# GLA recurrence and max-out MoE in one kernel: where w2·wo is summed, where unit 1's MoE stands, and how the last output is cut

## The chip, the cores and the metric

The kernel runs on one core of a Trainium2 chip. The metric is the time of one execution in device microseconds (us). Seven executions of the kernel before took 147.97 to 148.68 us, with a median of 148.49 us.

## What is computed

There are two stages. A gated recurrence runs over 768 time steps for 4 batches and 8 heads of 48 elements; its output, laid out as 3072 tokens of 384 elements, goes through a max-out block with 1024 hidden elements:

```python
for t in range(S):
    state = alpha[:, :, t, :, None] * state + np.einsum('bhd,bhe->bhde', k[:, :, t], v[:, :, t])
    y[:, :, t] = np.einsum('bhd,bhde->bhe', q[:, :, t], state)
x = y.transpose(0, 2, 1, 3).reshape(B * S, H * D)
out = np.maximum(x @ w1, x @ w2) @ w_out
```

All inputs and the output are float32.

## The kernel before

**Units.** The 3072 tokens are cut into 12 units of 256 tokens: unit u is block d = u // 4 of batch b = u % 4, and it holds two chunks (cc = 0, 1) of 128 tokens. Units 0 and 1 load q, k and v in another layout than the rest (`PAIRED`), which makes their loads fewer and some of their operations different. A unit's recurrent state comes from unit u - 4, so units 0 to 3 begin without one.

**The recurrence of a unit** goes through these helpers, each of which issues instructions at once on the engines named:

- `ln` (L190, ACT): the logarithm of alpha into one of three tiles `lg`.
- `sumd`, `sumc` (L215, L227, PE): sums over tokens of those logarithms, by matmuls with masks, into two PSUM tiles `cs` (tags g0, g1).
- `expm`, `expp`, `expd` (ACT): exponentials of the sums, into `Em`, back into `cs`, and into `de`.
- `kmul` (POOL) and `qmul` (DVE): k times `Em`, q times `cs`.
- `turn` (L291, PE, then a DVE copy at L301 or L303 into `qk`): eight 128x128 transposes for each chunk.
- `kvmm` (L305, PE), `kvsum` (DVE), `state` (POOL): the state's update.
- `pmm` (L338, PE) into two tiles `pp`, `pmask` (L347, DVE): the products of k and q in a chunk, and the causal mask over them, out of PSUM into `pt`.
- `ystate`, `yin` (PE), with two copies into `xn` on ACT (L388): the unit's output.
- `vcast` (L197): v to fp16, two casts on POOL (L205), two on ACT (L207), in units 0 and 1 two more on POOL (L209).

**The MoE of a unit.** max(h1, h2) is computed as relu(h1 - h2) + h2. So w12 = w1 - w2 is made once in quarters (`wsub`, L474, DVE), and w2o = w2 @ w_out is made once: `wcast` (L470, ACT and POOL) turns the two halves of w_out into fp16 `wo16`, `wturn` transposes w2, `wmul` (L455, 12 matmuls for each half of the hidden elements) sums into three PSUM tiles `wqs`, and `wout` (L466, three ACT copies) stores it. A unit then needs

- `xturn` (L390): six transposes and a DVE copy into `xt` (L399);
- `hid(u, f2)` (L401) for f2 = 0 to 3: six matmuls of 256 columns (L410) into a PSUM tile, and a relu into `gT`, on ACT (L415) or DVE (L417);
- `outp(u, n)` (L419) for each half n of 128 tokens: `outx`, three matmuls of 384 columns (x times w2o, L429), and `outg`, eight of 384 columns (`gT` times `wo16`, L436), then an ACT copy into `outs` (L439) and the store.

`dummies` (L478) issues matmuls on zeros, which no result uses.

**What sets the order.** `tc.manual_schedule()` (L484): from there each engine executes its instructions in the order of the calls, L487 to L640. Waits for data and for buffers are put in by the framework. An instruction that waits holds back everything behind it on its engine. All loads and stores are issued by SyncE (SP) in one queue, in order of the calls.

**Buffers.** PSUM has eight banks: tags m and pp with two each, g0 to g3 with one each. Tag m serves `dummies`, `wturn`, `hid`, `outx` and two of the three `wqs`; g0 and g1 serve `cs` and `turn`, g2 and g3 `kvmm`, `ystate`/`yin` and `xturn`. A tile on a tag waits until the readers of the tile before it are done.

**The order around the change** (L529 to L640): unit 0's `xturn`; unit 1's `turn`, `pmm`, `pmask` with `wmul(0)`, `wmul(1)` and `wout` between; the four `hid` of unit 0, with `wsub` and `dummies` between; `vcast(1)`; `ln(2)`; `outp(0, 0)`; unit 1's state, `sums(2)`, `exps(2)`; `outp(0, 1)`; unit 1's output, `turn(2)`, `xturn(1)`, `vcast(2)`, the four `hid` of unit 1, `ln(3)`. Then a loop over u = 2 to 11, where from u = 3 on the MoE of unit u - 1 stands between the steps of unit u; in the pass u = 2 only `outp(1, 0)` and `outp(1, 1)` do. The MoE of unit 11 follows the loop.

Of the kernel before, what the change touches and what calls it, by code (L numbers as in the profile page):

```python
# [8 lines left out]
FP16 = mybir.dt.float16  # L9
FP32 = mybir.dt.float32  # L10
# [5 lines left out]
def kernel(  # L16
# [27 lines left out]
    nc = tc.nc  # L44
    B, H, S, D = q.shape
    C = 128
    HP = H // 2
    P64 = 64
    ND2 = S // (2 * C)
    NU = B * ND2  # L50
    NT, DM = out.shape
    DFF = moe_w1.shape[1]
    NF = DFF // 128
# [12 lines left out]
    st = {}  # L66
# [33 lines left out]
    def load(u):  # L100
        load_a(u)
        if u in PAIRED:
            load_fat(u, "kf", k)
            load_fat(u, "qf", q)
        else:
            load_kq(u, 0)
            load_kq(u, 1)
        load_v(u)
# [77 lines left out]
    def new(tag, shape, dtype, bufs, name):  # L186
        return psp.tile(shape, dtype, tag=tag, bufs=bufs, name=name)


    def ln(u):  # L190
        X = st[u]
        X["lg"] = LG[u % NB]
        nc.scalar.activation(  # L193
            out=X["lg"][:, :, :, 0:D], in_=X["af"].rearrange("p h j d -> p j h d"), func=ACTF.Ln
        )
# [94 lines left out]

    def turn(u, cc):  # L291
        X = st[u]
        tp = new(f"g{cc}", [128, 2, HP, C], FP16, 1, "tp")
        for n, src in ((1, X["kn"][cc]), (0, X["qn"][cc])):
            for j in range(HP):
                nc.tensor.transpose(tp[:, n, j, :], pair(src, j), ident)  # L296
        if cc == 0:
            X["qk"] = gp.tile([128, 2, 2 * HP, C], FP16, tag="qk", bufs=2, name="qk")
        if u in PAIRED:
            o = X["qk"].rearrange("p c n (j t) -> p j n c t", j=2)[:, cc]  # L300
            nc.vector.tensor_copy(out=o, in_=tp.rearrange("p n h (c t) -> p (n h) c t", c=2))  # L301
        else:
            nc.vector.tensor_copy(out=X["qk"][:, cc], in_=tp.rearrange("p n h t -> p (n h) t"))  # L303
# [34 lines left out]
    def pmm(u, cc):  # L338
        X = st[u]
        qk = X["qk"][:, cc].rearrange("p (n h) t -> p n h t", n=2)  # L340
        X["pa", cc] = pa = [new("pp", [128, HP, C], FP32, 2, "pp") for _ in range(2)]
        for j in range(HP):
            for a in range(2):
                r = slice(64 * a, 64 * a + D)
                nc.tensor.matmul(pa[a][:, j, :], lhsT=qk[r, 1, j, :], rhs=qk[r, 0, j, :], start=True, stop=True)  # L345

    def pmask(u, cc):  # L347
        X = st[u]
        pt = X["pt", cc] = gp.tile([128, 2, HP, C], FP16, tag="pt", name="pt")
        for a in range(2):  # L350
            nc.vector.tensor_mul(  # L351
                out=pt[:, a], in0=X["pa", cc][a], in1=um.unsqueeze(1).to_broadcast([128, HP, C])
            )
# [36 lines left out]
    def xturn(u):  # L390
        X = st[u]
        xp = new("g2", [128, ND, 2, C], FP16, 1, "xp")
        for cc in range(2):
            xf = X["xn"][:, cc].rearrange("p j a d -> p (j a d)")
            for ds in range(ND):
                o = xp[:, ds].rearrange("p j (c t) -> p c j t", c=2)[:, cc]
                nc.tensor.transpose(o, xf[:, ds * 128 : (ds + 1) * 128], ident)  # L397
        X["xt"] = mp.tile([128, ND, 2, C], FP16, tag="xt", bufs=3, name="xt")
        nc.vector.tensor_copy(out=X["xt"], in_=xp)  # L399

    def hid(u, f2, on_act=None):  # L401
        X = st[u]
        if f2 == 0:
            X["gT"] = mp.tile([128, NF, 2 * C], FP16, tag="gT", name="gT")
        gT = X["gT"]
        hp = new("m", [128, 2, 2 * C], FP32, 2, "hp")
        for n in range(2):
            f = 2 * f2 + n
            for ds in range(ND):
                nc.tensor.matmul(  # L410
                    hp[:, n, :], lhsT=w12[:, ds, f * 128 : (f + 1) * 128],
                    rhs=X["xt"][:, ds].rearrange("p n t -> p (n t)"), start=(ds == 0), stop=(ds == ND - 1),
                )
        if f2 != 3 if on_act is None else on_act:
            nc.scalar.activation(out=gT[:, 2 * f2 : 2 * f2 + 2, :], in_=hp, func=ACTF.Relu)  # L415
        else:
            nc.vector.tensor_relu(out=gT[:, 2 * f2 : 2 * f2 + 2, :], in_=hp)  # L417

    def outp(u, n):  # L419
        outx(u, n)  # L420
        outg(u, n)
# [6 lines left out]
        for ds in range(ND):  # L428
            nc.tensor.matmul(op, lhsT=X["xt"][:, ds, n, :], rhs=w2o[:, ds, :], start=(ds == 0), stop=False)  # L429

    def outg(u, n):
        X = st[u]
        d, b = divmod(u, B)
        op = X["op"]
        for f in range(NF):
            nc.tensor.matmul(  # L436
                op, lhsT=X["gT"][:, f, n * C : (n + 1) * C], rhs=wo16[:, f, :], start=False, stop=(f == NF - 1)
            )
        nc.scalar.copy(out=X["outs"][:, n, :], in_=op)  # L439
        t0 = b * S + d * 2 * C  # L440
        dst = out[t0 : t0 + 2 * C, :].rearrange("(p j) d -> p j d", j=2)
        if u == NU - 1:
            nc.sync.dma_start(out=dst[:, n], in_=X["outs"][:, n])
        elif n == 1:
            nc.sync.dma_start(out=dst, in_=X["outs"])

    def wturn(ds):
        wt = new("m", [128, NF, 128], FP16, 2, "wt")
# [3 lines left out]

    wqs = []

    def wmul(n):  # L455

        if n == 0:
            wqs.extend([new("m", [128, DM], FP32, 2, "wq") for _ in range(2)] + [new("g3", [128, DM], FP32, 1, "wq")])
        for ds in range(ND):
            for f in range(4 * n, 4 * n + 4):  # L460
                nc.tensor.matmul(  # L461
                    wqs[ds], lhsT=w2T[:, f, ds * 128 : (ds + 1) * 128], rhs=wo16[:, f, :],
                    start=(f == 0), stop=(f == NF - 1),
                )

    def wout():  # L466
        for ds in range(ND):
            nc.scalar.copy(out=w2o[:, ds, :], in_=wqs[ds])

    def wcast(n):  # L470
        nc.scalar.copy(out=wo16[:, 4 * n : 4 * n + 2], in_=wof[:, 4 * n : 4 * n + 2])
        nc.gpsimd.tensor_copy(out=wo16[:, 4 * n + 2 : 4 * n + 4], in_=wof[:, 4 * n + 2 : 4 * n + 4])

    def wsub(n):  # L474
        f = slice(n * DFF // 4, (n + 1) * DFF // 4)
        nc.vector.tensor_sub(out=w12[:, :, f], in0=w1f[:, :, f], in1=w2f[:, :, f])

    def dummies(n):  # L478

        warm = new("m", [128, 512], FP32, 2, "warm")  # L480
        for _ in range(n):
            nc.tensor.matmul(warm, lhsT=wz[:, 0:128], rhs=wz, start=True, stop=True)  # L482
# [44 lines left out]
    qmul(1, 0)  # L527
    qmul(1, 1)
    xturn(0)  # L529
    turn(1, 0)  # L530
    dummies(2)
    turn(1, 1)
    wcast(0)
    pmm(1, 0)
    pmask(1, 0)
    wmul(0)
    wcast(1)
    wsub(0)
    pmm(1, 1)
    pmask(1, 1)  # L540
    wmul(1)
    wout()

    load(3)
    hid(0, 0, True)
    wsub(1)
    hid(0, 1, True)
    wsub(2)
    dummies(2)
    hid(0, 2, True)  # L550
    wsub(3)
    dummies(2)
    vcast(1)
    hid(0, 3, True)
    load(4)
    ln(2)
    outp(0, 0)
    kvmm(1, 0)
    kvmm(1, 1)
    kvsum(1, 0)  # L560
# [1 line left out]
    kvsum(1, 1)  # L562
    sums(2)
    exps(2)
    outp(0, 1)
    for cc in range(2):
        kmul(2, cc)
    for cc in range(2):
# [2 lines left out]
    yin(1)  # L571
    turn(2, 0)
    turn(2, 1)
    dummies(1)
    xturn(1)
    dummies(1)
    vcast(2)
    for f2 in range(4):
        hid(1, f2)
    ln(3)  # L580
    load(5)


    for u in range(2, NU):
        nxt = u + 1 < NU
        if u + 4 < NU:
            load(u + 4)
        kvmm(u, 0)
        pmm(u, 0)
        kvsum(u, 0)  # L590
        pmask(u, 0)
        state(u, 1)
        if more(u):
            kvmm(u, 1)
        if u > 2:
            hid(u - 1, 0)
            hid(u - 1, 1)
            if nxt:
                sumd(u + 1)
            hid(u - 1, 2)  # L600
        else:
            outp(1, 0)
            sumd(u + 1)
        if nxt:
            sumc(u + 1)
            expm(u + 1, 0)
            expp(u + 1, 0)
            expm(u + 1, 1)
        if more(u):
            kvsum(u, 1)  # L610
        pmm(u, 1)
        ystate(u)
        pmask(u, 1)
        if u > 2:
            hid(u - 1, 3, True)
        if nxt:
            expp(u + 1, 1)
            expd(u + 1)
            for cc in range(2):
                kmul(u + 1, cc)  # L620
                qmul(u + 1, cc)
            state(u + 1, 0)
        outp(u - 1, 0 if u > 2 else 1)
        yin(u)
        if nxt:
            turn(u + 1, 0)
            turn(u + 1, 1)
        if u > 2:
            outx(u - 1, 1)
        xturn(u)  # L630
        if nxt:
            vcast(u + 1)
        if u + 2 < NU:
            ln(u + 2)
        if u > 2:
            outg(u - 1, 1)
    for f2 in range(4):
        hid(NU - 1, f2)
    outp(NU - 1, 0)
    outp(NU - 1, 1)  # L640

# [1 line left out]
_INS = ['q', 'k', 'v', 'alpha', 'moe_w1', 'moe_w2', 'moe_w_out']  # L643
# [26 lines left out]
```

## Time and profile before

| what | us |
|---|---|
| median of 7 executions | 148.49 |
| the profiled execution, its own time | 148.6 |
| its span, first to last instruction | 146.9 |
| PE busy in the span | 136.3 (93%) |
| ACT, DVE, POOL busy | 97.2, 87.4, 56.5 |
| matmuls on zeros (L482, 33 of them) busy | 11.4 |
| first `kvmm` of the passes u = 2, 3, 4, 5 | 42.25, 49.91, 59.88, 69.64 |
| the last quarter of w1 lands | 27.40 |
| last matmul ends / last store issued / landed | 143.50 / 144.03 / 145.89 |

Lines of the timeline give the start and the length of a group of instructions on an engine, the engine, the source line, the operation, what it writes and reads, its size and how often it stands there; in brackets stands the idle time of the engine before it and what ended it. Matmuls overlap, so that a group's length holds the last one's way through the array (about 0.16 us after the next one could start). The chain of waits follows the end of the execution back from one instruction to what released it.

### The profile page before, as it was taken

Reading aid. Unit: us, or ns where it says so; the run is one execution under the profiler, and the core shown is the slowest. Engines: PE = TensorE matmul, PEld = TensorE weight load, DVE = VectorE, ACT = ScalarE, POOL = GpSimd, SP = SyncE. Lnnn points to the kernel's source line nnn. Section 1 sums busy time; section 2 is a strip of 40 time slices with the busy share of each in tenths; the row PEclk is TensorE's granted clock in tenths of the full one; section 3 lists DMA queues with packets and bytes.
Section 4 is the critical chain, followed back from the end, with each engine's and each line's share of the span. In section 5 each row is a group of like instructions: output and inputs, shape, how many; then the busy total and the mean of one; then the engine's idle time right before and its main releaser. Section 6 shows DMA issues by size and latency. Waiting matters only on the chain.

```text
span 146.9 us, 4239 instructions
## 1 busy us (share of the span) xinstructions
PE 136.3 (93%) x1681; PEld 97.6 (66%) x1681; DVE 87.4 (60%) x180; ACT 97.2 (66%) x199; POOL 56.5 (38%) x111
## 2 busy tenths in 40 slices
PE   6849978999899999999999999999999999998990
PEld 2335645666776787767877777678777777775750
DVE  6046988904648876756767867566675756570010
ACT  3467452777566878688687886887879768654511
POOL 7491252055405438154181371541913617310000
PEclk9995999999999999999999999999999999999999
DMA  4999999969969995799899999969969969120202
GB/s 111 270 372 306 311 365 341 224 115 220 178 117 258 158 286 100 145 220 168 178 285 159 283 170 240 224 111 262 197 112 278 171 116 345 61 107 4 107 12 95
DMA packets 76339, 28.58 MB, mean 195 GB/s; under 512 B 71712, under 2 KB 74528, under 8 KB 76320
## 3 DMA queue, kind: packets, MB, share of 16 engines
q1 hardware_dynamic: 76320, 28.32, 83.4%
q8 instruction: 13, 0.21, 0.6%
q14 instruction: 6, 0.05, 0.1%
HBM read 23.59 MB, written 4.72 MB: 193 GB/s over the span
## 4 chain that ended last, share of the span: by engine, by line
PE 86%; ACT 4%; DVE 4%; DMA 3%; issue 1%
PE hp L410 23%; PE op L436 21%; PE op L429 8%; PE tp L296 7%; PE pp L345 5%; PE cs L237 4%; PE wq L461 3%; PE ya L381 3%; PE warm L482 3%; DMA af<-in_alpha_dram 3%; PE xp L397 3%; PE kv L318 2%; DVE qk L303 2%; PE cs L223 2%; PE ya L369 1%; ACT cs L252 1%
## 5 line engine op out<-in xcount | busy, mean ns | idle before, releaser
L410 PE MATMUL hp<-xt,w 128*128 128x256 f16 x288 | 37.2, 273 | 0.8 <-DVE xt L399 0.6
L415 ACT ACTIVATE gT<-hp 128x512 f16<-128x512 f32 x46 | 27.4, 596 | 14.4 <-PE hp L410 13.7
L351 DVE TENSOR_TENSOR pt<-pp,um 128x512 f16<-128x512 f32 x48 | 30.9, 686 | 9.3 <-PE pp L345 8.8
L436 PE MATMUL op<-wo,gT 128*128 128x384 f16 x192 | 35.1, 326 | 0.0
L285 POOL TENSOR_TENSOR kn<-kf,Em 128x384 f16<-128x384 f32 x24 | 23.4, 997 | 23.7 <-ACT Em L247 23.7
L410 PEld LDWEIGHTS <-w 128*128 128x128 f16 x288 | 26.1, 97 | 6.1 <-issue 2.2
L436 PEld LDWEIGHTS <-gT 128*128 128x128 f16 x192 | 18.4, 98 | 11.3
L277 POOL TENSOR_TENSOR sb<-tm,dd 128x192 f16<-128x192 f32 x20 | 10.1, 506 | 38.2 <-DVE tm L331 23.4
L439 ACT COPY outs<-op 128x384 f32<-128x384 f32 x24 | 11.5, 478 | 16.9 <-PE op L436 16.7
L289 DVE TENSOR_TENSOR qn<-qf,cs 128x384 f16<-128x384 f32 x24 | 12.3, 550 | 12.2 <-ACT de L257 12.2
L331 DVE TENSOR_TENSOR tm<-kv,sb 64x192 f32<-64x192 f32 x32 | 11.3, 353 | 9.1 <-PE kv L318 6.9
L429 PE MATMUL op<-w2o,xt 128*128 128x384 f16 x72 | 15.6, 326 | 0.0
L303 DVE COPY qk<-tp 128x1024 f16<-128x1024 f16 x20 | 12.9, 686 | 4.3 <-PE tp L296 4.3
L205 POOL CAST v<-vf 64x384 f16<-64x384 f32 x24 | 12.0, 501 | 6.5 <-DMA vf<-in_v_dram 5.7
L247 ACT ACTIVATE Em<-cs 128x384 f32<-128x384 f32 x24 | 11.6, 485 | 4.0 <-PE cs L237 4.0
L207 ACT CAST v<-vf 64x384 f16<-64x384 f32 x24 | 12.2, 510 | 1.4 <-DMA vf<-in_v_dram 0.9
L482 PE MATMUL warm<-wz 128*128 128x512 f16 x33 | 11.4, 452 | 1.3 <-DVE halves L149 1.3
L193 ACT ACTIVATE lg<-af 128x768 f16<-128x768 f32 x12 | 10.1, 843 | 3.3 <-DMA af<-in_alpha_dram 3.1
L252 ACT ACTIVATE cs<-cs 128x384 f32<-128x384 f32 x24 | 11.8, 493 | 0.0
L296 PE MATMUL tp<-ident,kn 128*128 128x128 f16 x96 | 9.2, 218 | 2.0 <-DVE qn L289 2.0
L345 PE MATMUL pp<-qk 48*128 48x128 f16 x192 | 9.8, 221 | 0.8 <-DVE qk L301 0.8
L388 ACT CAST xn<-ya 128x384 f16<-128x384 f32 x24 | 10.4, 492 | 0.1
(60 smaller groups left out, 152.6 us busy)
## 6 DMA issues: line engine op xcount, KB each, us to landing
af<-in_alpha_dram SPq DMA_DIRECT2D x12, 384.0 KB, 6.2
vf<-in_v_dram SPq DMA_DIRECT2D x12, 384.0 KB, 4.8
out_dram<-outs SPq DMA_DIRECT2D x11, 384.0 KB, 5.2
kf<-in_k_dram SPq DMA_DIRECT2D x40, 96.0 KB, 4.5
qf<-in_q_dram SPq DMA_DIRECT2D x40, 96.0 KB, 4.1
w2f<-in_moe_w_dram SPq DMA_DIRECT2D x3, 512.0 KB, 5.9
wof<-in_moe_w_out_dram SPq DMA_DIRECT2D x2, 768.0 KB, 7.6
w1f<-in_moe_w_dram SPq DMA_DIRECT2D x4, 384.0 KB, 9.6
```

Source lines behind the costliest of these rows:

```text
L252: nc.scalar.activation(out=X["csv"][cc], in_=X["csv"][cc], func=ACTF.Exp)
L285: nc.gpsimd.tensor_mul(out=X["kn"][cc][:, :, 0:D], in0=part(u, "kf", cc), in1=X["Em"][cc])
L289: nc.vector.tensor_mul(out=X["qn"][cc][:, :, 0:D], in0=part(u, "qf", cc), in1=X["csv"][cc])
L296: nc.tensor.transpose(tp[:, n, j, :], pair(src, j), ident)
L303: nc.vector.tensor_copy(out=X["qk"][:, cc], in_=tp.rearrange("p n h t -> p (n h) t"))
L345: nc.tensor.matmul(pa[a][:, j, :], lhsT=qk[r, 1, j, :], rhs=qk[r, 0, j, :], start=True, stop=True)
L351: nc.vector.tensor_mul(out=pt[:, a], in0=X["pa", cc][a], in1=um.unsqueeze(1).to_broadcast([128, HP, C]))
L410: nc.tensor.matmul(hp[:, n, :], lhsT=w12[:, ds, f * 128 : (f + 1) * 128], rhs=X["xt"][:, ds].rearrange("p n t -> p (n t)"), start=(ds == 0 ...
L415: nc.scalar.activation(out=gT[:, 2 * f2 : 2 * f2 + 2, :], in_=hp, func=ACTF.Relu)
L429: nc.tensor.matmul(op, lhsT=X["xt"][:, ds, n, :], rhs=w2o[:, ds, :], start=(ds == 0), stop=False)
L436: nc.tensor.matmul(op, lhsT=X["gT"][:, f, n * C : (n + 1) * C], rhs=wo16[:, f, :], start=False, stop=(f == NF - 1))
L482: nc.tensor.matmul(warm, lhsT=wz[:, 0:128], rhs=wz, start=True, stop=True)
```

## The change

- `wqs` go on the tags g0, g1 and g3, and unit 0's `turn` on g2 and g3 in place of g0 and g1.
- `wmul` can be called for one of the three 128-row blocks of w2o. `wmul(0)` now comes straight after unit 1's `turn`; the three blocks of `wmul(1)` stand after unit 1's first `pmm` and after the first two `hid` of unit 0.
- All four `wsub` come before unit 1's masks (`pmask`), on DVE. `wout` comes after the third `hid` of unit 0 on ACT. Unit 1's second `pmm` comes after the fourth `hid`.
- `ln(2)` is called after `outp(0, 0)` in place of before it. `outg` can be called for some of its eight matmuls; the second `outg` of unit 0 is cut in two, and its second half, with the ACT copy, comes after `xturn(1)` and before `vcast(2)`.
- The four `hid` of unit 1 move into the pass u = 2, which now has the form of the passes behind it; `ln(3)` is called in that pass, after the second `hid`.
- Eight matmuls on zeros (`dummies`) around this become five.
- In the last pass the second `outg` of unit 10 is cut in two, with `xturn(11)` between the halves.
- The last 128 tokens' output is made by column halves (`outlast`): 11 matmuls of 192 columns, an ACT copy and a store issued by ACT; then 11 more, a DVE copy and a store issued by SP.

```diff
     def turn(u, cc):
-        tp = new(f"g{cc}", [128, 2, HP, C], FP16, 1, "tp")
+        tp = new(f"g{cc if u else 2 + cc}", [128, 2, HP, C], FP16, 1, "tp")
...
+    def outlast(u, n):
+        X = st[u]
+        for e in range(2):
+            c = slice(e * DM // 2, (e + 1) * DM // 2)
+            op = new("m", [128, DM // 2], FP32, 2, "oq")
+            for ds in range(ND):
+                nc.tensor.matmul(op, lhsT=X["xt"][:, ds, n, :], rhs=w2o[:, ds, c], start=(ds == 0), stop=False)
+            for f in range(NF):
+                nc.tensor.matmul(
+                    op, lhsT=X["gT"][:, f, n * C : (n + 1) * C], rhs=wo16[:, f, c], start=False, stop=(f == NF - 1)
+                )
+            if e == 0:
+                nc.scalar.copy(out=X["outs"][:, n, c], in_=op)
+                nc.scalar.dma_start(out=dst(u)[:, n, c], in_=X["outs"][:, n, c])
+            else:
+                nc.vector.tensor_copy(out=X["outs"][:, n, c], in_=op)
+                nc.sync.dma_start(out=dst(u)[:, n, c], in_=X["outs"][:, n, c])
...
-        if n == 0:
-            wqs.extend([new("m", [128, DM], FP32, 2, "wq") for _ in range(2)] + [new("g3", [128, DM], FP32, 1, "wq")])
+        if not wqs:
+            wqs.extend(new(f"g{i}", [128, DM], FP32, 1, "wq") for i in (0, 1, 3))
...
     xturn(0)
+    wcast(0)
+    dummies(2)
     turn(1, 0)
+    turn(1, 1)
     dummies(2)
-    turn(1, 1)
-    wcast(0)
-    pmm(1, 0)
-    pmask(1, 0)
     wmul(0)
     wcast(1)
     wsub(0)
-    pmm(1, 1)
-    pmask(1, 1)
-    wmul(1)
-    wout()
+    pmm(1, 0)
+    wmul(1, (0,))
     load(3)
     hid(0, 0, True)
     wsub(1)
+    wmul(1, (1,))
     hid(0, 1, True)
     wsub(2)
-    dummies(2)
+    wmul(1, (2,))
     hid(0, 2, True)
     wsub(3)
-    dummies(2)
+    pmask(1, 0)
+    wout()
+    dummies(1)
+    hid(0, 3, True)
     vcast(1)
-    hid(0, 3, True)
     load(4)
+    pmm(1, 1)
+    pmask(1, 1)
+    outp(0, 0)
     ln(2)
-    outp(0, 0)
...
-    outp(0, 1)
+    outx(0, 1)
+    outg(0, 1, (0, 1, 2, 3))
...
     turn(2, 1)
-    dummies(1)
     xturn(1)
-    dummies(1)
+    outg(0, 1, (4, 5, 6, 7))
     vcast(2)
-    for f2 in range(4):
-        hid(1, f2)
-    ln(3)
     load(5)
...
-        if u > 2:
-            hid(u - 1, 0)
-            hid(u - 1, 1)
-            if nxt:
-                sumd(u + 1)
-            hid(u - 1, 2)
-        else:
-            outp(1, 0)
+        hid(u - 1, 0)
+        hid(u - 1, 1)
+        if u == 2:
+            ln(3)
+        if nxt:
             sumd(u + 1)
+        hid(u - 1, 2)
...
-        if u > 2:
-            outx(u - 1, 1)
-        xturn(u)
+        outx(u - 1, 1)
         if nxt:
+            xturn(u)
             vcast(u + 1)
-        if u + 2 < NU:
-            ln(u + 2)
-        if u > 2:
+            if u + 2 < NU:
+                ln(u + 2)
             outg(u - 1, 1)
+        else:
+            outg(u - 1, 1, (0, 1, 2, 3))
+            xturn(u)
+            outg(u - 1, 1, (4, 5, 6, 7))
     for f2 in range(4):
         hid(NU - 1, f2)
     outp(NU - 1, 0)
-    outp(NU - 1, 1)
+    outlast(NU - 1, 1)
```

More of the change, by code (lines that the diff above doesn't have):

```diff
@@ L429, in outx, with outg @@
             nc.tensor.matmul(op, lhsT=X["xt"][:, ds, n, :], rhs=w2o[:, ds, :], start=(ds == 0), stop=False)
-    def outg(u, n):
+    def outg(u, n, fs=tuple(range(NF))):
         X = st[u]
-        d, b = divmod(u, B)
         op = X["op"]
-        for f in range(NF):
+        for f in fs:
             nc.tensor.matmul(
@@ L438, in outg, with dst @@
             )
-        nc.scalar.copy(out=X["outs"][:, n, :], in_=op)
-        t0 = b * S + d * 2 * C
[L441 to L445, printed above, removed]
+        if fs[-1] == NF - 1:
+            nc.scalar.copy(out=X["outs"][:, n, :], in_=op)
+            if u == NU - 1:
+                nc.sync.dma_start(out=dst(u)[:, n], in_=X["outs"][:, n])
+            elif n == 1:
+                nc.sync.dma_start(out=dst(u), in_=X["outs"])
+    def dst(u):
+        d, b = divmod(u, B)
+        t0 = b * S + d * 2 * C
+        return out[t0 : t0 + 2 * C, :].rearrange("(p j) d -> p j d", j=2)
+    def outlast(u, n):
[15 more added lines that the diff above has]
+                nc.sync.dma_start(out=dst(u)[:, n, c], in_=X["outs"][:, n, c])
     def wturn(ds):
@@ L453, with wmul @@
     wqs = []
-    def wmul(n):
-        if n == 0:
-            wqs.extend([new("m", [128, DM], FP32, 2, "wq") for _ in range(2)] + [new("g3", [128, DM], FP32, 1, "wq")])
-        for ds in range(ND):
+    def wmul(n, dss=(0, 1, 2)):
+        if not wqs:
+            wqs.extend(new(f"g{i}", [128, DM], FP32, 1, "wq") for i in (0, 1, 3))
+        for ds in dss:
             for f in range(4 * n, 4 * n + 4):
@@ L613 @@
         pmask(u, 1)
-        if u > 2:
-            hid(u - 1, 3, True)
+        hid(u - 1, 3, True)
         if nxt:
@@ L622 @@
             state(u + 1, 0)
-        outp(u - 1, 0 if u > 2 else 1)
+        outp(u - 1, 0)
         yin(u)
@@ L627 @@
             turn(u + 1, 1)
-        if u > 2:
-            outx(u - 1, 1)
-        xturn(u)
+        outx(u - 1, 1)
         if nxt:
+            xturn(u)
             vcast(u + 1)
-        if u + 2 < NU:
-            ln(u + 2)
-        if u > 2:
+            if u + 2 < NU:
+                ln(u + 2)
             outg(u - 1, 1)
+        else:
+            outg(u - 1, 1, (0, 1, 2, 3))
+            xturn(u)
+            outg(u - 1, 1, (4, 5, 6, 7))
     for f2 in range(4):
```

## The prediction

> **What bounds the kernel now.** First the page: its slices (3.67 us each), then the chain of waits by engine.
>
> ```profile
> PE   6849978999899999999999999999999999998990
> ...
> PEclk9995999999999999999999999999999999999999
> ...
> PE 86%; ACT 4%; DVE 4%; DMA 3%; issue 1%
> ```
>
> PE is the bound, 86% of the chain, and it is full but for the start and the end. Next, PE's timeline at the head of successive passes, and around the change:
>
> ```profile
> 33.09 0.70 PE L312 MATMUL kv<-v,kn 64*128 64x96 f16 x16
> 33.72 0.35 PE L223 MATMUL cs<-halves,lg 128*128 128x4 f16 x8
> ...
> 38.45 0.38 PE L482 MATMUL warm<-wz 128*128 128x512 f16 x1
> 39.44 2.97 PE L410 MATMUL hp<-xt,w 128*128 128x256 f16 x24 [0.61 <-DVE xt L399]
> 42.25 0.33 PE L318 MATMUL kv<-v,kn 128*128 128x96 f16 x4
> ```
>
> ```profile
> 69.64 0.33 PE L318 MATMUL kv<-v,kn 128*128 128x96 f16 x4
> ...
> 79.41 0.33 PE L318 MATMUL kv<-v,kn 128*128 128x96 f16 x4
> ```
>
> From the pass u = 4 (59.88) on, passes follow every 9.77 us, later every 9.6, with no wait on PE. The change leaves these passes alone, and PE is full in them: a delay ahead of 59.88 is not made good in them, nor a gain lost. So I work out how the changed kernel reaches `kvmm(4, 0)`, and then the tail. Last, ACT, where the change moves most:
>
> ```profile
> 31.66 0.59 ACT L415 ACTIVATE gT<-hp 128x512 f16<-128x512 f32 x1
> 32.27 0.84 ACT L193 ACTIVATE lg<-af 128x768 f16<-128x768 f32 x1
> 33.19 0.48 ACT L439 COPY outs<-op 128x384 f32<-128x384 f32 x1
> ...
> 37.92 1.03 ACT L207 CAST v<-vf 64x384 f16<-64x384 f32 x2
> 40.30 1.25 ACT L415 ACTIVATE gT<-hp 128x512 f16<-128x512 f32 x2 [1.34 <-PE hp L410]
> ```
>
> The reader should see the order: `ln(2)` ahead of the copy of `outp(0, 0)`, and the v casts of unit 2 straight after `xn`. Both change places.
>
> **Rates.** Successive matmuls start 0.163 us apart at 384 columns (eight take 1.30, 43.52 to 44.81), 0.109 at 256, 0.055 at 128; a result is usable some 0.16 after the next matmul could start, and a signal to another engine takes 0.04 to 0.06 (to POOL 0.09 to 0.15). Operations last what their rows show: relu 0.60, `ln` 0.85, `outs` copy 0.48, v cast 0.51.
>
> **Part 1, up to `sums(2)`.** Up to `xturn(0)` (19.80) the orders are equal; unit 0's earlier transposes gain 0.2 at 8.76 that later waits absorb. Then PE: two matmuls on zeros, both `turn`; DVE copies `qk` until 21.90 and 22.51. `wmul(0)` writes g0 and so waits for the first: 21.96 in place of 22.75, to 23.92. `pmm` to 24.34, the first block of `wmul(1)` to 24.99. `hid(0, 0)` needs the first `wsub`: that quarter of w1 lands at 23.97, DVE takes 0.95, so 25.02. The two other blocks and `hid` 1 and 2 follow closely to 28.29; the `wsub` are ready at 26.1, 27.2 and, from the last landing at 27.40, at 28.38. `hid(0, 3)` runs 28.73 to 29.38, after the one matmul on zeros. The masks of unit 1 now queue on DVE behind the last `wsub`: 28.30 to 29.59, and the second `pmm` needs their two PSUM tiles, so PE waits to 29.64 and goes on to 29.97. `wout` on ACT, behind the third relu, ends at 30.23, so `outx(0, 0)` ends at 30.44 and `outg` at 31.74, where before it was 33.0. **Gain here 1.25**, the three matmuls on zeros that go (0.22 each) included.
>
> It is not kept. `kvmm(1)` runs 31.84 to 32.47. Then `sums(2)` needs `ln(2)`, which now stands behind the copy of `outp(0, 0)`: copy 31.94 to 32.42, `ln` to 33.29, `sums(2)` at 33.34 against 33.72. Gain 0.38; PE idles 0.87.
>
> **Part 2, to `kvmm(2, 0)`.** `sums`, `outx` and four of the eight `outg` end at 35.20, `ystate` and `yin` at 35.9. In the old order the whole `outp(0, 1)` covered the exponentials; half of it does not. `de` ends 2.63 after `sums` start, 35.97, `qmul` at 36.56, `turn(2, 0)` at 36.61: PE idles 0.7. `turn(2, 1)` waits for the second `qmul` (37.08 to 37.52), `xturn(1)` to 37.86, the held-back half of `outg` to 38.51. That half hides the `xt` copy, which cost 0.61 before 39.44. But ACT now has unit 0's copy (38.71 to 39.19) ahead of `vcast(2)`, and `kvmm(2, 0)` needs the first of its two casts (39.21 to 39.72): it starts at 39.77. PE idles 1.26. Behind the waiting copy on ACT stand only these casts and the relus.
>
> **Part 3, the pass u = 2.** `kvmm`, `pmm`, `kvmm` as in a later pass: `hid(1, 0)` at 40.55, `hid(1, 1)` to 41.86. `sumd(3)` comes next and needs `ln(3)`, which on ACT is queued behind the relu of `hid(1, 1)`: relu 42.06 to 42.66, `ln` to 43.53, `sumd(3)` at 43.58. PE idles 1.72, and behind `sumd` wait `hid(1, 2)` and everything else. From `sumd` to the next pass take 7.57 (52.30 to 59.88 in the old pass u = 3): `kvmm(3, 0)` at 51.15, against 49.91. The old pass u = 3 held 0.31 of waiting for `xt`, the new one none, so it takes 9.66: `kvmm(4, 0)` at 60.81. **Up to here 0.93 is lost** (59.88 before). The loads keep their order on SP; the first store of unit 0 waits there for a copy that ends at 39.2, and was issued at 50.4.
>
> **Part 4, the tail.**
>
> ```profile
> 133.95 0.65 PE L429 MATMUL op<-w2o,xt 128*128 128x384 f16 x3
> 135.05 0.51 PE L397 MATMUL xp<-ident,xn 128*128 128x128 f16 x6 [0.45 <-ACT xn L388]
> 135.39 1.46 PE L436 MATMUL op<-wo,gT 128*128 128x384 f16 x8
> 136.69 3.05 PE L410 MATMUL hp<-xt,w 128*128 128x256 f16 x24
> 139.76 0.65 PE L429 MATMUL op<-w2o,xt 128*128 128x384 f16 x3
> ```
>
> Four `outg` (0.65) fill the 0.45 of waiting and push `xturn(11)` by only 0.04; `xt` is ready at 136.19, when the other four are done, and `hid(11, 0)` starts at 136.24 in place of 136.69. Through the relus, ACT's copy comes earlier too, and `outp(11, 0)` starts at 139.25 in place of 139.76: gain 0.50. `outlast`: 22 matmuls at 0.082 (between 0.055 and 0.109 by columns) take 1.80 against 1.79. The last result goes through a DVE copy of 192 columns (0.35, as `tm`) in place of 0.48, so the store goes out another 0.11 earlier. A store of 384 KB at the end lands in 2.30 us, one of 192 KB in 1.86. For 96 KB no row stands: between half of that, 0.93, and 1.86; the step from 384 to 192 continued gives 1.64. I take 1.70: gain 0.16. The store from ACT goes out at about 0.9 before it; no row shows a store from ACT, but it costs nothing unless it lands 0.9 later than one from SP, and it can gain nothing, not being last. Tail: -0.50 - 0.11 - 0.16 = **-0.77**.
>
> **Sum.** +0.93 - 0.77 = +0.16. The profiled execution took 148.6 us (span 146.9), which makes 148.76; it lay 0.11 above the median of 148.49, so as a median 148.65, say **148.7 us**. The waits of parts 1 to 3 are each read off within about 0.1, together 0.35, so this case reaches from 148.2 to 149.2.
>
> **The clock.** The windows view by stretches of 3.41 us (busy PE, weight load, DVE, ACT, POOL, then the granted clock, DMA share and rate):
>
> ```profile
> 7.55:10.96 3.41, 1.40 (x18) 1.08 (x18) 1.71 (x3) 2.24 (x6) 3.12 (x6) 1.00 1.09 379
> 10.96:14.37 3.41, 3.41 (x30) 1.91 (x28) 2.19 (x4) 2.48 (x3) 0.47 (x2) 0.50 1.16 311
> ...
> 21.20:24.61 3.41, 2.63 (x28) 1.57 (x25) 2.81 (x5) 0.83 (x1) 0.83 (x1) 1.00 1.10 349
> ```
>
> With PE busy for 1.40 us in one stretch the clock of the next was halved, though no single idle was over 1.2; with 2.63 it stayed. The changed kernel idles 1.26 and 1.72 within 5 us, and three matmuls on zeros are gone: some 3.41 there hold about 1.9 of busy PE, between the two. The Trainium skill ("TensorE: Matmul & The Clock Gate", "Why this matters for your kernels") asks only that no idle gap exceed about 3 us, by which the sum stays at 148.7. The row above contradicts that, since gaps of 1.2 sufficed; by the row, 150.4 is possible (below).
>
> **Rivals.**
> - *Slower, 149.2: the column halves give nothing.* After `outp(11, 0)`, where a weight load (row mean 98 ns) would pace the 192-column matmuls: 22 x 0.098 = 2.16, 0.36 more, and 96 KB land as late as 192, 0.16 more. The tail gives 0.25 and the net is +0.68. It decides from a spacing above 0.082. Against it: transposes load as many weights at 0.055.
> - *Slower, 150.4: one stretch at half clock* around 40 to 47, where PE is full: 3.41 / 2 = 1.7 on top. It decides where the busy share that halves the clock lies above some 55%.
> - *Faster, 147.9: the last store lands in proportion to its size*, 0.93, giving 0.77 more. Against it: 384 to 192 KB saved only 0.44 of 2.30.
> - *The change doesn't do what it says:* the moved `hid` hide nothing because ACT's order decides. This is in the forecast; without the wait for `ln(3)` it would be 1.7 less, but ACT takes its instructions in the order of the calls.
>
> **Chances.** Forecast 0.60, halves 0.18, clock 0.10, fast landing 0.12. About 0.2% (0.3 us) is what a measurement of this kernel can tell from no change. Of the forecast's 0.60, 0.34 lie within it, 0.20 above, 0.06 below. So faster 0.06 + 0.12 = 0.18, same 0.34, slower 0.20 + 0.18 + 0.10 = 0.48. The range 148.0 to 149.4 leaves out the clock and half of the fast landing.
>
> **What would show it.** `sums(2)` at about 33.3 behind `ln`; an idle of 1.3 before `kvmm(2, 0)` ended by a v cast; one of 1.7 before L223 near 43.6 ended by `ln`; `kvmm(4, 0)` near 60.8; `hid(11, 0)` straight behind `xt`, and the last store out 0.6 earlier relative to the last pass. I am wrong if `ln(3)` ends ahead of 42, if the clock row shows a second 5, or if the later passes are not 9.77 apart.

## The result, and the profile after

The changed kernel takes 148.85 us in the median of 12 executions (148.76 to 149.15); the kernel before, run beside it, 148.34 us (31 executions). The ratio is 1.0041, with a 95% interval of 1.0029 to 1.0053: slower by some 0.4%, clear of the 0.2% that the forecast gave as what can be told from no change. The forecast of 148.7 was 0.15 low, inside its range. The profiled execution took 148.76 us (span 147.0).

The engines are named PE (TensorE, the matmuls), ACT (ScalarE), DVE (VectorE), POOL (GpSimd) and SP (SyncE). The page of the changed kernel, slices of 3.68 us, then the chain by engine:

```profile
PE   6978879988659999999999999999999999999991
...
PEclk9999999999999999999999999999999999999999
...
PE 68%; SPq 25%; DMA 2%; issue 1%; ACT 1%; DVE 0%; ACTq 0%
```

Slices 9 to 12 of PE (8, 8, 6, 5: 29 to 44 us) are where it lost; they were 9, 9, 8, 9. Slice 37, an 8 before (the wait ahead of `xturn(11)`), is a 9. The clock row has no second dip. The chain's 25% on SP's queue is not a bound, and shows how a chain can be misread: at 42.61 it steps from `ln(3)` on ACT to a load of q, which lands at 44.08 and which `ln` does not read. The waits themselves are in the timeline of PE, still of the changed kernel:

```profile
24.91 0.83 PE L410 MATMUL hp<-xt,w 128*128 128x256 f16 x6 [0.18 <-DVE w L498]
...
33.25 0.35 PE L223 MATMUL cs<-halves,lg 128*128 128x4 f16 x8 [0.80 <-ACT lg L193]
...
36.53 0.38 PE L296 MATMUL tp<-ident,kn 128*128 128x128 f16 x4 [0.55 <-DVE qn L289]
...
39.69 0.34 PE L318 MATMUL kv<-v,kn 128*128 128x96 f16 x4 [1.10 <-ACT v L207]
...
43.51 0.35 PE L223 MATMUL cs<-halves,lg 128*128 128x4 f16 x8 [1.56 <-ACT lg L193]
...
60.76 0.33 PE L318 MATMUL kv<-v,kn 128*128 128x96 f16 x4
```

The front was to be faster: `hid(0, 0)` starts at 24.91 against 27.09 before. By 33.25 the gain is down to 0.47 (`sums(2)` stood at 33.72). Three waits later the first `kvmm` of the pass u = 4 stands at 60.76 against 59.88. Of the last four waits three end with ACT, and ACT's timeline says why:

```profile
31.85 0.48 ACT L439 COPY outs<-op 128x384 f32<-128x384 f32 x1 [0.17 <-PE op L435]
32.35 0.84 ACT L193 ACTIVATE lg<-af 128x768 f16<-128x768 f32 x1
...
38.62 0.48 ACT L439 COPY outs<-op 128x384 f32<-128x384 f32 x1 [1.84 <-PE op L435]
39.13 1.04 ACT L207 CAST v<-vf 64x384 f16<-64x384 f32 x2
41.34 1.25 ACT L415 ACTIVATE gT<-hp 128x512 f16<-128x512 f32 x2 [1.16 <-PE hp L410]
42.61 0.84 ACT L193 ACTIVATE lg<-af 128x768 f16<-128x768 f32 x1
```

ACT is not short of time: it sat idle for 1.84 and 1.16 us, waiting for PE, with the instruction that PE needs next queued behind the one that waits. `ln` of unit 2 stands behind the copy of `outp(0, 0)`, the v casts behind the copy of `outp(0, 1)`, `ln` of unit 3 behind the relus of `hid(1, 0)` and `hid(1, 1)`.

At the end, first PE's timeline, then the stores after 136 us in the transfer view (what is written, the queue, KB each, us from issue to landing):

```profile
135.96 0.50 PE L397 MATMUL xp<-ident,xn 128*128 128x128 f16 x6
...
137.11 3.03 PE L410 MATMUL hp<-xt,w 128*128 128x256 f16 x24
...
141.95 0.41 PE L457 MATMUL oq<-w2o,xt 128*128 128x192 f16 x3
...
143.11 0.82 PE L459 MATMUL oq<-wo,gT 128*128 128x192 f16 x8
```

```profile
out_dram<-outs SPq DMA_DIRECT2D x1, 192.0 KB, 1.9
out_dram<-outs ACTq DMA_DIRECT2D x1, 96.0 KB, 1.7
out_dram<-outs SPq DMA_DIRECT2D x1, 96.0 KB, 1.6
```

`xturn(11)` has lost its wait of 0.45, and so `hid(11, 0)` comes earlier in the pass. The last 22 matmuls start 0.083 us apart, which makes 1.82 us, and the last store goes out at 144.35 and lands at 145.97.

### The profile page after: what moved, and what is told of

Its sections match the earlier page's. It is cut to its first block, busy times and chain, and to the rows that moved or that the text cites. A ratio compares the mean times of both kernels' runs of the same rounds, so it can differ in the third digit from the quotient of the medians.

```text
span 147.0 us, 4259 instructions
## 1 busy us (share of the span) xinstructions
PE 135.5 (92%) x1689; PEld 97.2 (66%) x1689; DVE 87.4 (59%) x180; ACT 97.2 (66%) x200; POOL 56.5 (38%) x111
## 4 chain that ended last, share of the span: by engine, by line
PE 68%; SPq 25%; DMA 2%; issue 1%; ACT 1%; DVE 0%; ACTq 0%
PE hp L410 20%; PE op L435 19%; SPq L75 10%; SPq L85 9%; PE op L429 7%; PE tp L296 5%; PE pp L345 4%; SPq L124 3%; PE ya L381 3%; PE cs L237 3%; PE xp L397 2%; DMA qf<-in_q_dram 2%; PE kv L318 2%; SPq L115 2%; SPq L121 1%
## 5 line engine op out<-in xcount | busy, mean ns | idle before, releaser
L415 ACT ACTIVATE gT<-hp 128x512 f16<-128x512 f32 x47 | 28.1, 597 | 18.1 <-PE hp L410 17.5
L435 PE MATMUL op<-wo,gT 128*128 128x384 f16 x184 | 34.0, 326 | 0.0
L435 PEld LDWEIGHTS <-gT 128*128 128x128 f16 x184 | 17.5, 98 | 10.5
L439 ACT COPY outs<-op 128x384 f32<-128x384 f32 x23 | 11.0, 478 | 15.4 <-PE op L435 15.4
L429 PE MATMUL op<-w2o,xt 128*128 128x384 f16 x69 | 15.0, 326 | 0.0
L504 PE MATMUL warm<-wz 128*128 128x512 f16 x30 | 10.4, 463 | 1.3 <-DVE halves L149 1.3
L296 PE MATMUL tp<-ident,qn 128*128 128x128 f16 x96 | 9.3, 219 | 0.9 <-DVE qn L289 0.9
```

Of the source, the lines that this page charges most:

```text
L435: nc.tensor.matmul(op, lhsT=X["gT"][:, f, n * C : (n + 1) * C], rhs=wo16[:, f, :], start=False, stop=(f == NF - 1))
```

## The experiments

A time given after "against" is that of the kernel before, on the same chip and beside it. Each edit is shown against the kernel before or the changed kernel, as named. My theory was the forecast's: the front loses some 0.9 us, in waits that ACT's order makes, and the tail gains some 0.75. The rivals were its own (column halves that give nothing, a half clock), and, once the result was in, that something else than these two terms lay behind the 0.5 us between the medians.

**1. The tail alone.** The kernel before, with the split `outg(10, 1)` and `outlast`:

```diff
+        if not nxt:
+            outg(u - 1, 1, (0, 1, 2, 3))
         xturn(u)
...
-        if u > 2:
+        if not nxt:
+            outg(u - 1, 1, (4, 5, 6, 7))
+        elif u > 2:
             outg(u - 1, 1)
...
-    outp(NU - 1, 1)
+    outlast(NU - 1, 1)
```

> The kernel before with the new tail alone: the second outg of unit 10 in two halves around xturn(11), and the last output by column halves. Theory A (the front loses some 0.9 us by three waits on PE, the tail gains 0.7 to 0.8, each in its own place): 0.7 to 0.8 us faster than before, some 147.6 us, hid(11, 0) straight behind xt, last store landed 0.7 earlier. Rival B (the tail gives little, and the loss of the whole change is mostly there, through the store issued by ACT): within 0.2 us of before or slower.

Measured: 147.46 (6 executions) against 148.57, ratio 0.9937 (0.9915 to 0.9959). Its profiled execution had the clock's dip at 11 us, as the one shown first of the kernel before. PE's timeline:

```profile
136.24 3.03 PE L410 MATMUL hp<-xt,w 128*128 128x256 f16 x24
```

This is the predicted 136.24 to the digit; the last store lands at 145.09 in place of 145.89, and the span is 146.17 against 146.89. So the tail is a gain of 0.72 in the span, by itself. The medians differ by more, 1.11, because the executions of the kernel before fall into two heaps (experiment 7) and those two medians do not lie in the same one; the profiles compare like with like.

**2. and 3. Its two parts.** Of the same diff, first only the split of `outg(10, 1)` (the expectation speaks of loads, but no load is split), then only `outlast`.

> The kernel before, with the loads of the last output's tile row split into two as in the change and nothing else. Theory A (the tail's first term: the last hidden product starts straight behind the transposes, 0.45 to 0.5 us earlier): 0.40 to 0.50 us less than the kernel before on the same chip. Rival B (the tail's gain lies in the column halves alone, the earlier product is given back at the accumulator's copy): within 0.1 us of the kernel before.

> The kernel before, with the last output by column halves and nothing else. Theory A (the halves let the first copy and store go ahead, the last store is 96 KB and lands in 1.62 instead of 1.86, and the copy behind the last product is shorter): 0.25 to 0.35 us less than the kernel before. Rival B (192 columns a product cost more than they let go ahead): no change or up to 0.3 us more. With the split alone the two gains should add up to the 0.7 to 0.8 us of the whole tail.

Split alone: 148.08 (10 executions) against 148.54, ratio 0.9966 (0.9941 to 0.9991). From the start of `sums(11)` to `hid(11, 0)` its trace has 16.20 us, the kernel before 16.66; to the end of the span it has 26.39 against 26.86: 0.47 gained, none of it given back. Halves alone: 147.95 (10 executions), ratio 0.9962 (0.9936 to 0.9988), where the interval is too wide to size it. The traces do: it starts `sums(11)` at 119.54 and its last store lands at 145.06; an execution of the kernel before with `sums(11)` at 119.55 (the second one of experiment 7) lands at 145.40. That is 0.34 at the landing and 0.26 in the span. 0.47 and 0.26 make 0.73, the whole tail's 0.72 (26.13 us from `sums(11)` to the end in experiment 1, 26.14 in the changed kernel). The rival of the column halves falls: they gain.

**4. The front alone.** The changed kernel with the tail of the kernel before, that is without the three edits of experiment 1.

> The changed kernel with the old tail (outp of unit 11 whole, outg of unit 10 whole behind xturn). Theory A: 0.7 to 0.8 us slower than the changed kernel, 149.5 to 149.7, which is 1.2 to 1.4 over the median of before (0.9 over those executions of before in which the clock is halved a second time around 11 us, as in the profile shown). Rival B: within 0.2 us of the changed kernel, or faster.

Measured: 149.69 (6 executions) against 148.57, ratio 1.0121 (1.0072 to 1.0170). Four of the six lie at 149.39 to 149.71 with full clock, two at 151.48 and 151.53 with a mean clock of 0.989. One stretch of 3.41 us at half clock in their span of 149.8 makes just that (1 - 0.5 x 3.41 / 149.8 = 0.989), and 1.7 us. These two executions cost 1.9 more than the four, near the clock rival's price. That the clock is the cause is likely and not shown, nor is the place of such a stretch: the profile fell on one of the four. The place matters, since a stretch at 11 us gives the kernel before about the same mean clock (0.988) and costs it some 0.5.

**5. and 6. The same kernel twice more,** to catch such an execution in a profile.

> The front of the change with the tail of the kernel before, once more with a profile. Theory (one stretch of 3.41 us at half clock in some executions): either span 147.6 to 148.1 with full clock from about 7 us on, or span 149.6 to 150.0 with one stretch of 3.41 us at half clock, and then the stretch ahead of it is the one with the waits of 34 to 44 us. Rival (the longer executions come from transfers): full clock throughout and a later landing of w1 or of a weight.

> As the run of the same kernel ahead of it: span 147.6 to 148.1 at full clock, or 149.6 to 150.0 with one stretch of 3.41 us at half clock behind a stretch with the waits of 34 to 44 us (theory); by the rival, a late landing at full clock.

Both came at full clock: 149.54 (span 147.8) and 149.65 (147.9), inside the first of the two ranges, with full clock from 5.34 and 6.44. Where the half-clock stretch of the other two lay stays open. What can be said is that the waits at 38 to 44 us do not do it by themselves. Of any 3.41 us in the front of these traces, the emptiest between 5 and 48 us, from 40.2 on, holds 1.85 of busy PE. In the changed kernel's profile one of the clock's own stretches lies just there (the same holds for experiment 6, from 40.58 on; the windows view: PE, weight load, DVE, ACT, POOL, then clock), and the next one kept the full clock. None of the changed kernel's 12 executions shows a half-clock stretch: their mean clocks are 0.997 or more, where one such stretch makes 0.988.

```profile
41.24:44.65 3.41, 1.85 (x25) 1.21 (x24) 1.50 (x4) 2.11 (x4) 0.21 (x1) 1.00 1.05 231
44.65:48.06 3.41, 3.41 (x53) 2.53 (x50) 2.01 (x4) 2.83 (x8) 2.40 (x3) 1.00 0.96 152
```

**7. The kernel before, twice more, with a profile.** Front and tail together account for the profiled executions. But the medians differ by 0.51. So I asked where the kernel before gets executions as short as 148.0, and the changed one none.

> The kernel before, unchanged, profiled once more. Theory A says that its time hangs on where the clock's stretches fall: with the clock halved around 11 to 14 us as in the profile shown, sums(2) starts at about 33.7 us and the span is about 146.9; without it the front is up to 0.8 us earlier and the span some 146.2 to 146.5. Rival B: the clock's row differs and the span does not follow it.

> The kernel before, unchanged, profiled a third time. Its executions fall into two groups, spans near 146.4 and near 146.9. Two profiles so far, both of the upper group: one with a second stretch at half clock around 11 us, one whose first stretch at half clock lasted to 6.8 us. If the phase of the clock's stretches makes the groups (theory A), an execution with the clock full from about 5 to 6 us and no second halving has sums(2) at about 33.2 and a span near 146.4; in the other case it repeats one of the two. Rival B: a span near 146.4 with the clock as in one of those two.

First: 148.52, span 146.82; second: 148.11, span 146.40. Neither has the second half-clock stretch. The first missed what I expected for that: its full clock began only at 6.79 us (5.72 in the second, 4.13 in the profile shown first), and a long half-clocked start costs as much as a late dip. PE's timeline of the second, at `sums(1)` and `hid(0, 0)`:

```profile
15.50 0.34 PE L223 MATMUL cs<-halves,lg 128*128 128x4 f16 x8
...
26.59 1.47 PE L410 MATMUL hp<-xt,w 128*128 128x256 f16 x12
```

| execution | full clock from | `sums(1)` | first w1 quarter lands | `hid(0, 0)` | span |
|---|---|---|---|---|---|
| before, shown first | 4.13, half 10.96 to 14.37 | 16.35 | 23.97 | 27.09 | 146.89 |
| before, first here | 6.79 | 15.93 | 24.00 | 27.02 | 146.82 |
| before, second here | 5.72 | 15.50 | 23.92 | 26.59 | 146.40 |
| changed | 7.11 | 15.32 | 23.87 | 24.91 | 147.05 |
| front alone, experiment 4 | 5.09 | 15.32 | 24.08 | 25.12 | 147.98 |
| front alone, experiment 5 | 5.34 | 15.50 | 23.93 | 24.97 | 147.84 |
| front alone, experiment 6 | 6.44 | 15.49 | 24.05 | 25.09 | 147.94 |

In the kernel before, `hid(0, 0)` varies by 0.5 us with the start, and the span with it: span less `hid(0, 0)` is 119.80, 119.80 and 119.81. Without the dip it comes 11.10 us after `sums(1)`, with the dip 10.74, because waits behind `sums(1)` then shrink. Experiments 1 to 3, which have the same front, agree: 10.74 with a dip (27.09), 11.09 without (26.49 and 26.60, full clock from 4.23 and 5.67). In the changed front `hid(0, 0)` comes 1.04 us after w1's first quarter every time, whenever `sums(1)` ran, in experiments 8 to 11 too. The executions of the kernel before beside these experiments fall into two heaps, 17 of 41 at 148.01 to 148.21 and 20 at 148.54 to 148.81 (four lie elsewhere). The six of the 41 whose mean clock shows the dip (0.988) are all in the upper heap. The 12 executions of the changed kernel lie at 148.76 to 149.15, in one heap.

**8. ACT's order, all three waits.** The changed kernel with `ln(2)` ahead of `outp(0, 0)`, the v casts and `ln(3)` ahead of the held-back half of `outg`:

```diff
-    outp(0, 0)
     ln(2)
+    outp(0, 0)
...
-    outg(0, 1, (4, 5, 6, 7))
     vcast(2)
+    ln(3)
+    outg(0, 1, (4, 5, 6, 7))
...
-        if u == 2:
-            ln(3)
```

> The changed kernel with three calls moved so that ACT takes them earlier: ln(2) ahead of outp(0, 0), vcast(2) ahead of the second half of outg of unit 0, ln(3) straight behind vcast(2). Nothing else is changed. Theory A (three waits of PE of 0.8, 1.1 and 1.6 us in the changed kernel are made by ACT's order alone): all three shrink to 0.2 or less, 2.5 to 3.5 us less than the changed kernel, 145.4 to 146.4 us, under both kernels. Rival C (the waits are given back by the next thing that is late, the exponentials, xt or the loads): less than 1 us gained, 148 us or more.

Measured: 146.72 (145.93 to 147.53, 6 executions) against 148.57, ratio 0.9882 (0.9848 to 0.9916): 2 us less than the changed kernel, and a smaller gain than I expected. All three waits went as expected (the first to 0.17), but a new one took their place; PE's timeline, then ACT's:

```profile
32.60 0.35 PE L223 MATMUL cs<-halves,lg 128*128 128x4 f16 x8 [0.17 <-ACT lg L193]
...
37.77 0.33 PE L318 MATMUL kv<-v,kn 128*128 128x96 f16 x4
...
41.11 0.81 PE L410 MATMUL hp<-xt,w 128*128 128x256 f16 x6 [1.70 <-ACT outs L439]
```

```profile
39.85 0.84 ACT L193 ACTIVATE lg<-af 128x768 f16<-128x768 f32 x1 [1.74 <-DMA af<-in_alpha_dram]
40.60 0.46 ACT L439 COPY outs<-op 128x384 f32<-128x384 f32 x1
```

`ln(3)` stood so early that its alpha had not landed. Behind it on ACT waited the copy that frees a PSUM tile of tag m, and so the next `hid`. It is the same mechanism, with a transfer at its head.

**9. `ln(3)` alone, straight behind the v casts:**

```diff
     vcast(2)
+    ln(3)
...
-        if u == 2:
-            ln(3)
```

> The changed kernel with ln(3) called straight behind vcast(2) in place of behind the second hid of the pass u = 2; nothing else. Theory A: the wait of 1.56 us ahead of sumd(3) goes, if unit 3's alpha (landed at 38.6 to 40.1 so far) is there when ACT has finished the v casts at 40.2; the waits of 0.8 and 1.1 us before it stay. 1.5 us less than the changed kernel: 147.2 to 147.5. Rival C (given back): another wait of over 1 us stands in pass 2, 148.3 or more.

Measured: 147.01 (146.84 to 147.21, 4 executions) against 148.44, ratio 0.9907 (0.9887 to 0.9928); profiled 147.11, which is 1.65 below the changed kernel's 148.76. That is a little more than I expected. In PE's timeline `sumd(3)` has no wait left:

```profile
41.87 0.34 PE L223 MATMUL cs<-halves,lg 128*128 128x4 f16 x8
```

**10. The v casts alone,** `vcast(2)` ahead of the held-back half of `outg`.

> The changed kernel with vcast(2) called ahead of the held-back half of unit 0's outg; nothing else. Theory A: the wait of 1.1 us ahead of kvmm(2, 0) goes (unit 2's v landed at 36.5 to 37.5 so far, so the casts end at 38.3 at the latest), the one of 1.56 before sumd(3) stays as it is, since ln(3) follows the relus: 0.9 to 1.1 us less than the changed kernel, 147.7 to 148.0. Rival C: below 0.3 us.

Measured: 147.56 (147.44 to 147.84, 4 executions), ratio 0.9947 (0.9927 to 0.9967); profiled 147.49, 1.27 less than the changed kernel, and a little more gain than expected. In PE's timeline the wait before `kvmm(2, 0)` is gone, and the one behind it keeps its size and moves up:

```profile
38.36 0.33 PE L318 MATMUL kv<-v,kn 128*128 128x96 f16 x4
...
42.20 0.35 PE L223 MATMUL cs<-halves,lg 128*128 128x4 f16 x8 [1.56 <-ACT lg L193]
```

**11. The best order I found.** As experiment 8, but `ln(3)` behind the first `hid` of unit 1 and `sumd(3)` behind the third, so that ACT meets `ln(3)` after alpha has landed and PE has two `hid` to do meanwhile:

```diff
         hid(u - 1, 0)
-        hid(u - 1, 1)
         if u == 2:
             ln(3)
-        if nxt:
+        hid(u - 1, 1)
+        if nxt and u > 2:
             sumd(u + 1)
         hid(u - 1, 2)
+        if u == 2:
+            sumd(3)
```

> The changed kernel with ln(2) ahead of outp(0, 0), vcast(2) ahead of the held-back half of outg, and in the pass u = 2 ln(3) behind the first hid and sumd(3) behind the third. In the run with three calls moved, ln(3) stood on ACT ahead of unit 0's copy, and waited for alpha of unit 3 (39.83), so that PE waited 1.7 us for the PSUM tile which that copy frees. Here the copy is not behind ln(3). Theory A with that correction: the waits of PE in pass 2 sum to less than 0.6 us, kvmm(3, 0) near 48, 145.4 to 145.9 us with less spread than that run. Rival C: the loads hold it, 146.5 or more.

Measured: 146.10 (145.59 to 146.75, 6 executions) against 148.44, ratio 0.9843 (0.9816 to 0.9869). It beats both kernels, the one before by 1.6% and the changed one by 1.9% of their medians, though not by as much as I expected. The pass u = 2 went as expected, with `kvmm(3, 0)` at 47.99. What is left is the `qmul` wait of 0.53 at 36.0, and a wait one pass later, again for a copy on ACT, which stands behind an `ln` that waits 0.91 for its alpha (PE's timeline):

```profile
50.21 0.82 PE L410 MATMUL hp<-xt,w 128*128 128x256 f16 x6 [0.62 <-ACT outs L439]
```

## Why the prediction was right, and the step that failed

| step | predicted | measured in the changed kernel's trace |
|---|---|---|
| `hid(0, 0)` | 25.02 | 24.91 |
| `sums(2)`, idle before it | 33.34, 0.87 | 33.25, 0.80 |
| `turn(2, 0)` | 36.61, 0.7 | 36.53, 0.55 |
| `kvmm(2, 0)` | 39.77, 1.26 | 39.69, 1.10 |
| `sumd(3)` | 43.58, 1.72 | 43.51, 1.56 |
| `kvmm(3, 0)`, `kvmm(4, 0)` | 51.15, 60.81 | 51.09, 60.76 |
| front, against 59.88 | +0.93 | +0.88 |
| from `kvmm(4, 0)` to `sums(11)`, 60.15 before | no change | 60.15 |
| `outp(11, 0)` earlier, counted from `sums(11)` | -0.50 | -0.47 |
| 22 matmuls of 192 columns | 1.80 | 1.82 |
| end of the last matmul to last store | -0.11 | -0.11 (0.42 for 0.53) |
| landing of 96 KB | 1.70 | 1.62 |
| last landing to end of span | no change | 1.08 for 1.00 |
| the profiled execution | 148.76 | 148.76 |
| from there to the median | -0.11 | +0.09 |

**Front.** Every wait came where it was put, behind the instruction that was named. The marks are 0.05 to 0.11 early as one block, from `hid(0, 0)` on; the profile's waits are 0.07 to 0.16 shorter than my idle, which I counted from when the next matmul could have started, and the profile from the end of the record before. Experiments 9 and 10 show that ACT's order is the cause of the last two waits, ahead of `kvmm(2, 0)` and `sumd(3)`, and not merely beside them. Moving one call in ACT's queue takes away that wait alone; without the wait for `ln(3)`, which the forecast priced at 1.7, the profiled time falls by 1.65. The wait ahead of `sums(2)` went when `ln(2)` moved, but that call was only moved together with others (experiments 8 and 11). The wait for `qmul` is not one of ACT's order: it stands at 0.53 to 0.55 in experiments 8 to 11 alike. The forecast laid it to the exponentials, which half of `outp(0, 1)` no longer covers; no run moves that half back.

**Tail.** The two terms are additive and of the predicted sizes (experiments 1 to 3). One cost was missed: the span ends 1.07 to 1.08 us after the last landing in all of the kernels with `outlast`, and 1.00 to 1.01 in all without. The store from ACT, which the forecast took to cost nothing, may be the reason, but what part of `outlast` does it is not shown. With the 0.05 of the front and 0.03 of the tail's other terms, it explains how the sum could meet 148.76 to the digit: three small errors cancelled, which is luck. One step of its range does not follow either: 0.35 of error in the waits reaches from 148.35 to 149.05 around 148.7, and not from 148.2 to 149.2. The measured 148.85 lies in both.

**The step that failed is the last one:** "it lay 0.11 above the median of 148.49, so as a median 148.65". That took the profiled execution's distance from the median as scatter that any kernel of this kind would share. It was not. The execution shown belonged to the longer heap of the kernel before, and the median lies among two heaps, 0.45 us apart (spans of 146.4 and 146.9). The start of `hid(0, 0)` makes the difference (experiment 7): before, it hung on how soon PE was through its first work up to `sums(1)`, which depends on where the clock's stretches fall. In the changed front it waits for w1, so a lucky start gains nothing there. The right step was to carry over nothing: 148.76, against a median of 148.85. (In that profile w1's first quarter landed at 23.87, earlier than in the three profiles of experiments 4 to 6, 23.93 to 24.08, which fits a median a little above it.) The two heaps are most of why the medians differ by 0.51 where the profiled executions differ by 0.16.

**The rivals.** The column halves giving nothing (0.18) falls: a spacing of 0.083, the 0.082 of the forecast, where the rival needed 0.098, and a landing of 1.62, where it needed 1.86. The landing in proportion to size (0.12) falls by the same 1.62, against 0.93. The clock (0.10) did not come in 12 executions of the changed kernel. In two of six of its front alone the mean clock points to it, at about the price given (1.9 for 1.7), but no profile caught it. That the moved `hid` hide nothing because of ACT's order was part of the forecast, and holds.

## What to carry to other kernels

Where each engine takes its instructions in order, read for every moved instruction what it now stands behind on its engine, and whether that one waits for the busiest engine: an engine idle for a third of the span cost the whole gain here, and moving four calls by a few lines (experiment 11) took 2.3 us off the profiled time. An instruction moved too far forward fails in the same way, behind a load that has not landed. And before a profiled execution's distance from the median is carried over, find out whether the kernel's times come in heaps, what makes them, and whether the changed kernel still depends on it.

## What the runs showed of the hardware

- **The clock.** After a stretch of 3.41 us with PE busy for 1.40, the next ran at half clock (before); so it did after 1.49 in the same place of the tail-only kernel. After one with 1.56, in the same place of the split-only kernel, it did not, nor after 1.85 in the changed kernel. The windows of the tail-only kernel, then of the split-only kernel, columns as above:

```profile
7.67:11.08 3.41, 1.49 (x19) 1.19 (x20) 1.71 (x3) 2.24 (x5) 3.12 (x6) 1.00 1.08 382
11.08:14.49 3.41, 3.41 (x32) 1.91 (x31) 2.39 (x4) 2.43 (x4) 0.36 (x2) 0.50 1.16 307
...
7.64:11.05 3.41, 1.56 (x19) 1.25 (x20) 1.71 (x3) 2.23 (x5) 3.10 (x6) 1.00 1.09 380
11.05:14.46 3.41, 3.01 (x47) 1.80 (x45) 2.73 (x5) 2.42 (x4) 0.31 (x2) 1.00 1.16 310
```

  So in these traces the line lies between 44% and 46% of busy PE, and not at the 55% from which the forecast's clock rival would have decided. No single gap in the halved cases exceeded 1.2 us. The Trainium skill ("TensorE: Matmul & The Clock Gate", "Why this matters for your kernels") asks for no idle gap over about 3 us. These traces show that to be too mild.
- **The phase of the clock's stretches** against the start of the kernel differed between the executions profiled (first full clock at 4.1 to 7.1 us in the thirteen profiles that record it), and moved the kernel before by some 0.45 us, 0.3% of it. The same page ("Part 1: The HAM clock gate") says that the window runs freely and shifts the transition from run to run. The traces agree; here the shift was as large as the effect that was to be measured.
- **Small stores at the end** land in 1.62 us for 96 KB from SP, 1.68 for 96 KB from ACT, 1.85 for 192 KB and 2.31 for 384 KB: halving the size again saved 0.23, after 0.46.
